# Transposing the attention weights on TensorE, redividing PSUM for the sums, and moving one normalisation past the MLP weight loads, in a one-core Trainium2 transformer block

## The chip, the core and the metric

The kernel runs on one NeuronCore of a Trainium2 chip. The engines are named as the profile names them: PE is TensorE (PEld its weight loads), DVE is VectorE, ACT is ScalarE, POOL is GpSimd, and SP is SyncE, which here only issues DMA transfers. Each engine works through its own queue in order, and semaphores tie the queues together. The metric is the device time of one execution in microseconds (us).

## The reference

The block is a pre-norm attention layer with softmax feature maps (linear attention), followed by an MLP whose input is normalised twice. S = 2048 rows, D = 576, H = 32 heads of width 18, F = 4608, all in bf16.

```python
def _A_ref(x, wqkv, w_phi, wo):
    qkv = (x @ wqkv) -> q, k, v per head
    pq = einsum("bhsd,hdf->bhsf", q, w_phi);  pk = the same of k
    phi_q = concat([softmax(pq), softmax(-pq)]);  phi_k = the same of pk
    kv = einsum("bhsf,bhsd->bhfd", phi_k, v);  z = einsum("bhsf->bhf", phi_k)
    num = phi_q @ kv;  den = phi_q . z + 1e-6
    return (num / den) @ wo

def _B_ref(x, w1, b1, w2, b2):
    y = layernorm(x)
    return gelu(y @ w1 + b1) @ w2 + b2

h  = x + _A_ref(layernorm(x), ...)
h2 = h + _B_ref(layernorm(h), ...)
```

## The kernel before

The 2048 rows are 16 tiles of 128 (`t`), four to a block `b`. The 32 heads are in 5 groups `g` of 7, 7, 7, 7 and 4 heads, that is of 126 (the last of 72) columns. PE and POOL run in the order in which the program writes their work, to the end of the kernel; ACT, DVE and SP do so up to `front.close()`, after which a planner orders them.

**Weights and normalisation (0 to about 17 us).** `x` comes in four loads. `wv`, the value weights, is loaded by `load_rows`: rows on partitions, in two transfers, and a third of a row (1152 bytes) at a time. The key and query weights are needed with their columns on partitions, because `fold` multiplies them by `bd`, a block-diagonal matrix of the head maps `w_phi` that POOL builds in `spread`. `load_turned` therefore loads them as `wkT` and `wqT` with five transposing DMAs each. `fold` makes `wkp` and `wqp`, the weights with the head maps multiplied in, one 128-row chunk `c` per call: six matmuls into a PSUM tile `pW`, then one copy to SBUF. `measure` takes the mean and variance of a tile on DVE (`bn_stats` twice, `bn_aggr`, and the one-column step `va`) and the inverse root `rs` on POOL; `scale` writes the normalised rows `lnb` on DVE. Tiles 0 to 3 are turned on PE (`transpose_to`), tiles 4 to 15 by a DMA on SP's queue, into `lnT`.

**The key loop (about 17 to 69 us).** For each tile `key` is ten matmuls into `pk`, two exponentials on ACT (`phik`), and a sum and a reciprocal on DVE (`sk`, `rk`). `value` is ten matmuls into `pv` and one copy on ACT (`vf`). `weigh` makes `vs` = `vf` * `rk` twice (for the two signs), on POOL, and for sign 0 of the last two tiles on DVE. From tile 6 on, each step also holds one `ask`: five matmuls of 512 columns for one (block, group) of the queries into `pq`, and two exponentials on ACT (`eT`). There are 20 asks. In the loop are also the two stages of `fold` for the query weights (at t = 3 and 4), and the measuring and scaling of later tiles.

**Sums and attention chain (about 69 to 102 us).** `sums(g, s)` accumulates over the 16 tiles into `pkv`; two DVE instructions (L405, L411) mask it into `kvm`. `combine(t, u)` takes tile t and one of two units of groups (0 to 2, or 3 and 4): matmuls into `pn`, two small copies on ACT (`sw`), a product on DVE (`tt`), a sum on POOL (`uu`), and, when its returned function is called, a division on DVE (`rec`, `ob`). `turn`, `residual`, `rescale` and `turn2` take a finished tile through the output projection (`pa`), the residual, the two normalisations and a transpose into `ln2T`.

**The MLP.** Eight slices of 256 rows; each is 324 matmuls into `ph` with `w1` (`up`), then four accumulations of 36 matmuls into `po` with `w2` (`down`). The attention work of later tiles is hung between the `po` matmuls by a table of marks. Every `po` accumulation needs all of `w2`; its first 18 matmuls use quarters 0 and 2, its last 18 quarters 1 and 3.

**Memory.** In PSUM the pool `two` has three buffers of two banks (`pw`, `pW`, `pk`, `pv`, `pkv`, `pn`, `pa`) and `one` has two buffers of one bank (`pT`, `pq`, `pb1`) until the MLP begins. In SBUF, `w1` and `w2` (41.5 KB per partition each) begin where the pool `kpool` lay, with all `phik` (36.9 KB) and `vs` (38.9 KB). So `w1` can be loaded once `sums(4, 1)` has read these, and `w2` reaches about 7 KB beyond, into the place of `tf_pool`, where the `tt` tiles of the first five `combine` calls lie; the last of these is `d20 = combine(2, 0)`. The loads are eight transfers of `w1` (L575; each fills 64 partitions) and then four of `w2` (L578; 128 partitions), all on SP's queue.

Of the kernel before, what the change touches and what calls it, by code (L numbers as in the profile page):

```python
# [8 lines left out]
P = 128  # L9
# [6 lines left out]
D = 576  # L16
# [21 lines left out]
def kernel(  # L38
# [65 lines left out]
    wkT = wpool.tile([P, NG, D], BF16, name="wkT", tag="wkT")  # L104
    wqT = wpool.tile([P, NG, D], BF16, name="wqT", tag="wqT")
# [4 lines left out]
    lnb = [wpool.tile([P, DP], BF16, name=f"lnb{i}", tag=f"lnb{i}") for i in range(4)]  # L110
# [5 lines left out]
    def load_turned(dst, first):  # L116
        for g in range(NG):
            f0 = first + g * 126
            nc.sync.dma_start_transpose(dst[:, g : g + 1, :], A_wqkv[:, f0 : f0 + P])

    wphi_rows = A_w_phi.rearrange("h d f -> (h d) f")
# [5 lines left out]
    nc.sync.dma_start(xh[:, 1:4, :], x_v[:, 1:4, :])  # L127
    load_rows(wv, A_wqkv[:, 2 * D : 3 * D])
    nc.sync.dma_start(xh[:, 4:8, :], x_v[:, 4:8, :])
    load_turned(wkT, D)  # L130
    load_turned(wqT, 0)
# [16 lines left out]
    nc.vector.memset(wv[64:P, 4, :], 0.0)  # L148
    for i in range(4):
        nc.vector.memset(lnb[i][:, D:DP], 0.0)  # L150
# [20 lines left out]
    def inverse(mv, n, bias, scale):  # L171
        va = small.tile([P, 2], FP32, name="va", tag="va")
        nc.vector.tensor_scalar(va[:, 0:n], mv[:, 0:n, 1], scale, bias, ALU.mult, ALU.add)  # L173
        rs = small.tile([P, 2], FP32, name="rs", tag="rs")
        nc.gpsimd.tensor_tensor(rs[:, 0:n], va[:, 0:n], mhalf[:, 0:n], ALU.pow)  # L175
        return rs

    def statistics(tiles, bias, scale):
        n = len(tiles)
        mv = small.tile([P, 2, 2], FP32, name="mv", tag="mv")  # L180
        for i, t in enumerate(tiles):
            st = small.tile([P, 2, nc.vector.BN_STATS_DIM], FP32, name="st", tag="st")
            nc.vector.bn_stats(st[:, 0, :], xh[:, t, 0:HALF])
            nc.vector.bn_stats(st[:, 1, :], xh[:, t, HALF:D])
            nc.vector.bn_aggr(mv[:, i, :], st[:, :, :])
        return mv, inverse(mv, n, bias, scale)
# [9 lines left out]
    def measure(*tiles):  # L196
        mv, rs = statistics(tiles, EPS, 1.0)
        for i, t in enumerate(tiles):
            moments[t] = (mv, rs, i)
# [5 lines left out]
    def scale(t):  # L205
        normalise(lnb[t % 4][:, 0:D], xh[:, t, :], *moments[t])
        if t >= 4:
            nc.sync.dma_start_transpose(turned(t), lnb[t % 4][:, :])
# [14 lines left out]
    def fold(wT, wp, c, copy):  # L223
        m = P if c < NC - 1 else 64
        pW = two.tile([P, 2, 512], FP32, name="pW", tag="two")
        for i, off, g, lo, hi in BITS:
            k = P if g < NG - 1 else 72
            nc.tensor.matmul(
                pW[:m, i, off : off + hi - lo],
                wT[:k, g, c * P : c * P + m],  # L230
                bd[:k, g, :, :].rearrange("p h f -> p (h f)")[:, lo:hi],
                start=True, stop=True,
            )
        copy(wp[:m, c, 0:D].rearrange("p (i f) -> p i f", i=2), pW[:m, :, 0:HALF])

    eT = {}

    def ask(b, g):
        if g == 0:
            eT[b] = e_pool.tile([P, NG, 2, 512], BF16, name="eT", tag="eT")  # L240
        pq = one.tile([P, 512], FP32, name="pq", tag="one")
        for c in range(NC):
            nc.tensor.matmul(  # L243
                pq[:, :], wqp[:, c, g * 126 : g * 126 + P], lnT[b][:, c, :],
                start=(c == 0), stop=(c == NC - 1),
            )
        nc.scalar.activation(eT[b][:, g, 0, :], pq[:, :], AF.Exp, scale=1.0)
        nc.scalar.activation(eT[b][:, g, 1, :], pq[:, :], AF.Exp, scale=-1.0)  # L248
# [43 lines left out]
    warm(40)  # L292
# [4 lines left out]
    warm(8)  # L297
    measure(2)
    scale(1)
    transpose_to(lnb[1], turned(1))  # L300
    value(0)
    spread(0)
    measure(3)
    scale(2)
    transpose_to(lnb[2], turned(2))
    value(1)
    spread(1)
    spread(2)
    measure(4, 5)
    scale(3)  # L310
    transpose_to(lnb[3], turned(3))
    value(2)
    spread(3)
    spread(4)
    value(3)
    scale(4)
    scale(5)
    fold(wkT, wkp, 0, nc.scalar.copy)
    fold(wkT, wkp, 1, nc.vector.tensor_copy)
    fold(wkT, wkp, 2, nc.scalar.copy)  # L320
    fold(wkT, wkp, 3, nc.vector.tensor_copy)
    fold(wkT, wkp, 4, nc.scalar.copy)
# [4 lines left out]
    asked = iter([(b, g) for b in range(NT // 4) for g in range(NG)])  # L327
    for t in range(NT):
        key(t)
        if t == 0:  # L330
            scale(6)
            scale(7)
        if t in (3, 4):
            for c in ((0, 1), (2, 3, 4))[t - 3]:
                fold(wqT, wqp, c, nc.scalar.copy)
        if t >= 6:
            ask(*next(asked))
# [30 lines left out]
    more = lambda: ask(*next(asked))  # L368
    more()
    more()  # L370
    inner.close()

# [18 lines left out]

    def sums(g, s):
        n = GH[g]
        m = P if g < NG - 1 else n * DH
        pkv = two.tile([P, 7 * VW], FP32, name="pkv", tag="two")
# [20 lines left out]
    banks = {}  # L416

    def bank(shape, dtype, name):
        pool, tag = banks["one"]
        return pool.tile(shape, dtype, name=name, tag=tag)  # L420
# [56 lines left out]
    def residual(t):  # L477
        st = small.tile([P, 2, nc.vector.BN_STATS_DIM], FP32, name="st", tag="st")
        mv = small.tile([P, 2, 2], FP32, name="mv", tag="mv")
        for i in range(2):  # L480
            cs = slice(i * HALF, (i + 1) * HALF)
            pool, tag = banks["pa"]
            pa = pool.tile([P, HALF], FP32, name="pa", tag=tag)
            for c in range(NC):
                nc.tensor.matmul(  # L485
                    pa[:, :], oTs[t][:, c, :], wo[:, c, cs],
                    start=(c == 0), stop=(c == NC - 1),
                )
            nc.vector.tensor_tensor(xh[:, t, cs], pa[:, :], xh[:, t, cs], ALU.add)  # L489
            nc.vector.bn_stats(st[:, i, :], xh[:, t, cs])  # L490
# [8 lines left out]
    def turn2(t):  # L499
# [8 lines left out]
        for c0, c1 in ((0, 5), (5, KC)):  # L508
# [3 lines left out]
            copy = nc.vector.tensor_copy if c0 else nc.scalar.copy  # L512
            copy(dst[:, c0:c1, :], pT[:, 0 : c1 - c0, :])
# [6 lines left out]
    banks["one"] = (one, "one")  # L520
    banks["two"] = (two, "two")

    banks["pa"] = (two, "two")
    banks["tt"] = tf_pool

    sums(0, 0)
    sums(0, 1)
    sums(1, 0)
    sums(1, 1)
    sums(2, 0)  # L530
    sums(2, 1)
    sums(3, 0)
    d00 = combine(0, 0)
    sums(3, 1)
    d10 = combine(1, 0)
    d00()
    more()
    turn_b1()
    more()
    sums(4, 0)  # L540
    d10()
    sums(4, 1)
    kctx.close()
    d01 = combine(0, 1)
# [3 lines left out]
    more()  # L548
    more()
    turn(0)  # L550
    turn(1, nc.vector.tensor_copy)
    more()
    m0 = residual(0)
    m1 = residual(1)
    more()
    rescale(0, *m0)
    more()
    turn2(0)
    rescale(1, *m1)
    more()  # L560
    turn2(1)
    d20 = combine(2, 0)
    d20()
# [13 lines left out]
    for q in (0, 2, 1, 3):  # L577
        nc.sync.dma_start(w2[:, 9 * q : 9 * q + 9, :], w2v[:, 9 * q : 9 * q + 9, :])  # L578
    psA.close()
    front.close()  # L580

    pn_pool = ctx.enter_context(
        tc.tile_pool(name="pn_pool", bufs=1, space=bass.MemoryType.PSUM, reuse_waits="tile")
    )
    acc = ctx.enter_context(
        tc.tile_pool(name="acc", bufs=6, space=bass.MemoryType.PSUM, reuse_waits="tile")
    )
    banks["one"] = (acc, "acc")
    banks["two"] = (pn_pool, "pn")

    banks["pa"] = (acc, "acc")
# [70 lines left out]

    for s_ in range(NS):
        mlp(s_)
# [31 lines left out]
```

## Time and profile before

| | |
|---|---|
| median of three runs | 427.08 us (427.08 to 427.48) |
| the profiled execution | 426.47 us |
| its span, from the first instruction to the last | 424.8 us |
| busy share of PE / PEld / ACT / DVE / POOL | 94% / 77% / 45% / 43% / 25% |
| PE work of the two MLP products, `ph` and `po` | 143.1 and 151.1 us |
| DMA moved | 27.08 MB |

Two lines of the profile's table of 40 slices (10.6 us each) say where DMA counts; a digit is the busy share in tenths, and the second line is the rate in each slice:

```profile
DMA  9762140099990320121032004101210220030000
GB/s 218 138 156 40 34 110 0 2 189 208 256 346 9 71 46 3 29 58 32 2 57 60 3 3 85 31 2 29 59 31 3 56 63 3 2 71 15 2 2 28
```

DMA is busy in two places: in the first three slices, when inputs and attention weights arrive, and in slices 9 to 12 (85 to 127 us), when the MLP weights do. PE's clock is granted in full but for two stretches of 3.41 us, from 98.50 and from 129.22 us, in which it is at half.

### The profile page before, as it was taken

What the parts mean: (1) busy time and instruction counts of PE and PEld (TensorE: products, weight loads), DVE (VectorE), ACT (ScalarE), POOL (GpSimd) and SP (SyncE); (2) the same over time, 40 slices, a digit from 0 to 9 for tenths busy, and PEclk for the clock granted to TensorE, in tenths of its full rate; (3) what the DMA queues carried; (4) which work ended last, traced back from release to release, by engine and by line L of the source; (5) the groups of instructions that cost most, each with busy time, mean ns of one, the idle gap of its engine ahead of it and who ended that gap; (6) DMA issues with size and microseconds to landing.
All of it is one profiled execution on the core that took longest, in us unless ns stands there. A gap on an engine that the chain in (4) does not pass through costs nothing.

```text
span 424.8 us, 11023 instructions
## 1 busy us (share of the span) xinstructions
PE 400.6 (94%) x4811; PEld 325.9 (77%) x4811; DVE 182.1 (43%) x397; ACT 191.5 (45%) x460; POOL 106.2 (25%) x139
## 2 busy tenths in 40 slices
PE   7879998886988899999999999999999999999997
PEld 6656666744966688788888888887888888878875
DVE  6689998664024630750174046206601740330000
ACT  3678775255851148107601840481067018404810
POOL 5258798112011320141023004101410240011000
PEclk9999999998998999999999999999999999999999
DMA  9762140099990320121032004101210220030000
GB/s 218 138 156 40 34 110 0 2 189 208 256 346 9 71 46 3 29 58 32 2 57 60 3 3 85 31 2 29 59 31 3 56 63 3 2 71 15 2 2 28
DMA packets 53130, 27.08 MB, mean 64 GB/s; under 512 B 40026, under 2 KB 52698, under 8 KB 52954
## 3 DMA queue, kind: packets, MB, share of 16 engines
q1 hardware_dynamic: 52480, 26.36, 27.4%
q8 instruction: 37, 0.61, 0.6%
q10 hardware_dynamic: 602, 0.02, 0.1%
q14 instruction: 11, 0.09, 0.1%
HBM read 14.48 MB, written 2.36 MB: 40 GB/s over the span
## 4 chain that ended last, share of the span: by engine, by line
PE 80%; DMA 6%; DVE 5%; SPq 3%; ACT 2%; issue 1%; POOL 1%; DVEq 0%; ACTq 0%; POOLq 0%
PE po L629 32%; PE ph L602 29%; PE pa L485 4%; PE pq L243 4%; PE pv L253 4%; PE pk L253 4%; DMA w<-in_B_w_dram 3%; SPq L578 2%; PE pkv L397 2%; PE pn L434 2%; DMA xh<-in_A_x_dram 2%; DMA lnT<-lnb 1%; DVE tt L445 1%; DVE vs L286 1%; POOL uu L451 1%
## 5 line engine op out<-in xcount | busy, mean ns | idle before, releaser
L629 PE MATMUL po<-w,h 128*128 128x288 bf16 x1152 | 151.1, 288 | 3.7 <-DMA w<-in_B_w_dram 3.7
L608 ACT ACTIVATE h<-ph,b1col 128x256 bf16<-128x256 f32 x288 | 120.9, 471 | 72.0 <-PE ph L602 52.9
L602 PE MATMUL ph<-ln2T,w 64*128 64x256 bf16 x2592 | 143.1, 269 | 1.8 <-DVE tt L445 1.4
L602 PEld LDWEIGHTS <-w 64*128 64x128 bf16 x2592 | 126.8, 94 | 17.7 <-issue 3.7
L629 PEld LDWEIGHTS <-h 128*128 128x128 bf16 x1152 | 111.2, 98 | 32.8 <-issue 5.6
L489 DVE TENSOR_TENSOR xh<-pa,xh 128x288 bf16<-128x288 f32 x32 | 14.4, 449 | 110.6 <-PE pa L485 110.6
L175 POOL TENSOR_TENSOR rs<-va,mhalf 128x1 f32<-128x1 f32 (+1 forms) x26 | 15.5, 594 | 163.4 <-DVE va L173 163.1
L442 ACT COPY sw<-pn 128x21 f32<-128x21 f32 (+1 forms) x32 | 5.5, 173 | 98.9 <-PE pn L434 98.9
L451 POOL TENSOR_TENSOR uu<-tt 128x399 f32<-128x399 f32 (+1 forms) x32 | 26.4, 826 | 84.1 <-DVE tt L445 82.3
L253 PEld LDWEIGHTS <-lnT 128*128 128x128 bf16 x320 | 31.0, 98 | 12.2 <-DMA lnT<-lnb 2.5
L286 POOL TENSOR_TENSOR vs<-vf,rk 128x608 bf16<-128x608 bf16 x30 | 36.8, 1253 | 7.0 <-DVE rk L281 5.8
L633 DVE TENSOR_TENSOR ot<-po,hb 128x288 bf16<-128x288 f32 x32 | 14.5, 454 | 52.7 <-PE po L629 52.7
L445 DVE TENSOR_TENSOR tt<-pn,sw 128x798 f32<-128x798 f32 (+1 forms) x32 | 25.1, 786 | 22.9 <-ACT sw L443 22.8
L619 POOL TENSOR_TENSOR hb<-xh,b2bc 128x576 f32<-128x576 bf16 x16 | 20.4, 1272 | 53.2 <-DVE ot L633 53.2
L243 PE MATMUL pq<-lnT,wqp 128*128 128x512 bf16 x100 | 25.2, 389 | 1.8 <-ACT eT L248 1.1
L253 PE MATMUL pk<-wkp,lnT 128*128 128x288 bf16 x160 | 21.7, 286 | 2.3 <-DMA lnT<-lnb 2.3
L253 PE MATMUL pv<-wv,lnT 128*128 128x288 bf16 x160 | 22.1, 286 | 0.1
L485 PE MATMUL pa<-wo,oT 128*128 128x288 bf16 x160 | 22.1, 286 | 0.0
L272 ACT ACTIVATE phik<-pk 128x576 bf16<-128x576 f32 x32 | 19.1, 649 | 6.4 <-PE pk L253 6.0
L277 DVE TENSOR_REDUCE sk<-phik 128x64 f32<-128x1152 bf16 x16 | 21.2, 1327 | 0.1
L456 DVE TENSOR_TENSOR ob<-uu,rec 128x378 bf16<-128x378 f32 (+1 forms) x32 | 20.3, 633 | 1.1
L189 DVE TENSOR_SCALAR ln<-xh,mv,rs 128x576 bf16<-128x576 bf16 x32 | 16.8, 569 | 7.0 <-POOL rs L175 7.0
(70 smaller groups left out, 240.1 us busy)
## 6 DMA issues: line engine op xcount, KB each, us to landing
w<-in_B_w_dram SPq DMA_DIRECT2D x8, 648.0 KB, 15.7
w<-in_B_w_dram SPq DMA_DIRECT2D x4, 1296.0 KB, 16.2
out_dram<-ot SPq DMA_DIRECT2D x16, 144.0 KB, 1.8
xh<-in_A_x_dram SPq DMA_DIRECT2D x1, 1152.0 KB, 6.3
wv<-in_A_wqkv_dram SPq DMA_DIRECT2D x1, 576.0 KB, 6.2
xh<-in_A_x_dram SPq DMA_DIRECT2D x1, 576.0 KB, 6.8
wo<-in_A_wo_dram SPq DMA_DIRECT2D x1, 576.0 KB, 4.2
xh<-in_A_x_dram SPq DMA_DIRECT2D x1, 432.0 KB, 3.4
```

What stands on the lines that cost most here:

```text
L243: nc.tensor.matmul(pq[:, :], wqp[:, c, g * 126 : g * 126 + P], lnT[b][:, c, :], start=(c == 0), stop=(c == NC - 1),)
L253: nc.tensor.matmul(dst[:, i, 0:HALF], lhs[:, c, :], w[:, c, i * HALF : (i + 1) * HALF], start=(c == 0), stop=(c == NC - 1),)
L277: nc.vector.tensor_reduce(sk[:, :], phik[t][:, :, :].rearrange("p s (h f) -> p (s h) f", f=DH), AX.X, ALU.add)
L286: eng.tensor_tensor(vs[t][:, s, :, :], vf[t % 4][:, :, :], rk[t][:, s, :].rearrange("p (h o) -> p h o", o=1).to_broadcast([P, NH, VW]), AL ...
L445: nc.vector.tensor_tensor(tt[:, :, 0:nh, :], pnv[:, :, :, 0:VW], sw[:, :, 0:nh].rearrange("p s (h o) -> p s h o", o=1).to_broadcast([P, 2, ...
L451: nc.gpsimd.tensor_tensor(uu[:, 0:nh, :], tt[:, 0, 0:nh, :], tt[:, 1, 0:nh, :], ALU.add)
L456: nc.vector.tensor_tensor(o[:, h0 * DH : (h0 + nh) * DH].rearrange("p (h d) -> p h d", d=DH), uu[:, 0:nh, 0:DH], rec[:, 0:nh].rearrange("p ...
L485: nc.tensor.matmul(pa[:, :], oTs[t][:, c, :], wo[:, c, cs], start=(c == 0), stop=(c == NC - 1),)
L602: nc.tensor.matmul(ph[half][:, :], w1[rows, c, p_ * P : (p_ + 1) * P], x[rows, c, :], start=(c == 0), stop=(c == KC - 1),)
L608: nc.scalar.activation(h1[m // 9][:, m % 9, :], ph[half][:, :], AF.Gelu_apprx_tanh, bias=b1col[:, m : m + 1], scale=1.0,)
L619: nc.gpsimd.tensor_tensor(hb[:, :], xh[:, t, :], b2bc[:, :], ALU.add)
L629: nc.tensor.matmul(po[:, :], h1[m // 9][:, m % 9, i_ * P : (i_ + 1) * P], w2[:, m, cs], start=(n == 0), stop=(n == NM - 1),)
```

## The change

- The key and query weights are loaded by `load_rows`, as `wv` is, into two of the four `eT` buffers, which nobody needs so early. The order on SP's queue is x (tile 0), x (1 to 3), `wk`, `wv`, x (4 to 7), `wq`, x (8 to 15). A new function `flip` turns one group of columns on PE (five transposes into a PSUM tile of pool `two`) and copies it into one shared tile `wT`, on ACT or DVE.
- The order of the start is new: flips of `wk` stand between the transposes of the first tiles, folds between the values; the measuring of tiles 4 and 5 moves from before the scaling of tile 3 to after the last fold; `value(3)` moves to after `key(0)`. The five flips of `wq` stand at t = 1 and 2, its folds at t = 3 (three) and t = 4 (two). The first warm-up has 46 transposes in place of 40, the second (8) is gone. `lnb` has six buffers in place of four. From tile 4 on, the one-column step `va` is POOL's.
- After the key loop PSUM is divided anew: `pair_pool` (two buffers of two banks, for `pn`), `free_pool` (two of one bank, for `pkv`, `pT`, `pb1`, `pa`) and `ask_pool` (two of one bank, for `pq`).
- The order of sums, asks and combines is new: `combine(0, 0)` and `combine(1, 0)` come before `sums(3, 0)`, an ask before them; one ask is split round the `combine` of the second units; both `rescale` calls come together.
- `combine(2, 0)` moves from before the MLP weight loads to after them, past the twelve issues on SP's queue and past the closing of the PSUM pools; its `tt` then lies in `tt_pool`.

The core of the diff:

```diff
-    wkT = wpool.tile([P, NG, D], BF16, name="wkT", tag="wkT")
-    wqT = wpool.tile([P, NG, D], BF16, name="wqT", tag="wqT")
+    wT = wpool.tile([P, NG, D], BF16, name="wT", tag="wT")
...
+    load_rows(wk, A_wqkv[:, D : 2 * D])
     load_rows(wv, A_wqkv[:, 2 * D : 3 * D])
     nc.sync.dma_start(xh[:, 4:8, :], x_v[:, 4:8, :])
-    load_turned(wkT, D)
-    load_turned(wqT, 0)
+    load_rows(wq, A_wqkv[:, 0:D])
...
-    def inverse(mv, n, bias, scale):
+    def inverse(mv, n, bias, scale, eng=nc.vector):
-        nc.vector.tensor_scalar(va[:, 0:n], mv[:, 0:n, 1], scale, bias, ALU.mult, ALU.add)
+        eng.tensor_scalar(va[:, 0:n], mv[:, 0:n, 1], scale, bias, ALU.mult, ALU.add)
...
+    def flip(w, g, copy):
+        m = P if g < NG - 1 else 72
+        pX = two.tile([P, DP], BF16, name="pX", tag="two")
+        for c in range(NC):
+            nc.tensor.transpose(
+                pX[:m, c * P : (c + 1) * P], w[:, c, g * 126 : g * 126 + m], ident[:, :]
+            )
+        copy(wT[:m, g, :], pX[:m, 0:D])
...
+    warm(46)
     measure(0); measure(1); scale(0); transpose_to(lnb[0], turned(0))
+    flip(wk, 0, act); measure(2); scale(1); flip(wk, 1, dve)
+    transpose_to(lnb[1], turned(1)); spread(0..2)
+    flip(wk, 2, act); measure(3); scale(2); flip(wk, 3, dve)
+    transpose_to(lnb[2], turned(2)); flip(wk, 4, act); spread(3); spread(4)
+    value(0); scale(3); fold(wkp, 0, act); transpose_to(lnb[3], turned(3))
+    fold(wkp, 1, dve); value(1); fold(wkp, 2, act); fold(wkp, 3, dve)
+    value(2); fold(wkp, 4, act)
+    measure(4, 5); scale(4); scale(5); measure(6, 7)
...
     for t in range(NT):
         key(t)
         if t == 0:
             scale(6)
             scale(7)
+            value(3)
+        if t in (1, 2):
+            for g in ((0, 1, 2), (3, 4))[t - 1]:
+                flip(wq, g, act)
         if t in (3, 4):
-            for c in ((0, 1), (2, 3, 4))[t - 3]:
-                fold(wqT, wqp, c, nc.scalar.copy)
+            for c in ((0, 1, 2), (3, 4))[t - 3]:
+                fold(wqp, c, act)
...
+    psA.close()
+    pair_pool = psum_pool(psB, "pair_pool", 2)
+    free_pool = psum_pool(psB, "free_pool", 2)
+    ask_pool = psum_pool(psB, "ask_pool", 2)
...
     sums(0, 0) ... sums(2, 1)
-    sums(3, 0); d00 = combine(0, 0); sums(3, 1); d10 = combine(1, 0); d00()
-    more(); turn_b1(); more(); sums(4, 0); d10(); sums(4, 1)
+    more(); d00 = combine(0, 0); d10 = combine(1, 0); sums(3, 0); d00()
+    turn_b1(); sums(3, 1); d10(); more(); sums(4, 0); sums(4, 1)
     kctx.close()
...
-    d20 = combine(2, 0)
-    d20()
     fore.close()
...
+    combine(2, 0)()
     for s_ in range(NS):
         mlp(s_)
```

(Calls are put on one line here where the diff has one to a line.)

## The prediction

> **What bounds the kernel now.** I read the chain of waits first, backwards: which wait ends last in each stage. Its rows are start, length (us), engine, work, line.
>
> ```profile
> 65.18 1.19 ACT phik L272 x2
> ...
> 67.37 1.88 DVE vs L286
> ...
> 71.27 0.87 DVE vs L286
> 72.18 5.99 PE pkv L397 x97
> ...
> 105.00 0.39 SPq L578
> ...
> 115.37 13.83 DMA w<-in_B_w_dram
> 129.24 2.32 PE po L629 x9
> ```
>
> From 129.24 to the span's end at 424.8 the chain is almost all PE: 295.6 us in which the change alters nothing but names of pools. What releases PE at 129.24 is the last quarter of `w2`. Before that, the sums waited until 72.18 for DVE's last `vs`.
>
> Next, the busy times by stretches of 2 us: length, then PE, PEld, DVE, ACT, POOL, the clock, the DMA share and GB/s.
>
> ```profile
> 88.00:90.00 2.00, 1.21 (x12) 0.77 (x12) 0.96 (x3) 1.55 (x3) 0.00 (x0) 1.00 1.08 209
> ...
> 104.00:106.00 2.00, 2.00 (x40) 2.00 (x38) 0.96 (x2) 0.91 (x3) 2.00 (x2) 1.00 1.08 215
> ...
> 110.00:112.00 2.00, 2.00 (x42) 2.00 (x38) 0.00 (x0) 1.72 (x5) 0.00 (x0) 1.00 1.09 192
> ...
> 114.00:116.00 2.00, 1.60 (x31) 1.29 (x27) 0.00 (x0) 1.54 (x4) 0.00 (x0) 1.00 1.07 353
> ...
> 126.00:128.00 2.00, 0.00 (x0) 0.00 (x0) 0.76 (x3) 0.00 (x0) 1.02 (x1) 1.00 0.67 216
> ```
>
> The DMA engines are full from 88 to 126 without a hole. `w1` (576 x 4608 x 2 bytes = 5.31 MB) runs at about 205 GB/s, 26 us; then `w2`, as large, at 356, 15 us; with start and tail 44.7 us from the first issue (84.54, right after the last `pkv`) to 129.24. So the end is **t_w + 44.7 + 295.6**, where t_w is the moment at which `sums(4, 1)` frees `w1`'s place, as long as PE reaches the 19th matmul of the first `po` before the load does. It does: it stood there 3.3 us. Everything between t_w and that point goes into that wait.
>
> Last, the start, from the timeline of PE and ACT (in brackets: idle time before, and what ended it):
>
> ```profile
> 25.11 1.40 PE L253 MATMUL pk<-wkp,lnT 128*128 128x288 bf16 x10 [2.33 <-DMA lnT<-lnb]
> 26.54 1.19 ACT L272 ACTIVATE phik<-pk 128x576 bf16<-128x576 f32 x2 [2.01 <-PE pk L253]
> 27.62 1.70 ACT L234 CAST wqp<-pW 128x576 bf16<-128x576 f32 x3
> 27.78 0.44 PE L228 MATMUL pW<-bd,wqT 128*64 128x126 bf16 x6 [0.73 <-ACT phik L272]
> 28.32 1.39 PE L253 MATMUL pv<-wv,lnT 128*128 128x288 bf16 x10
> ```
>
> `key(4)` waits for a DMA that stood on SP's queue behind ten transposing loads; then a third `pW` waits for a buffer of `two` until ACT has done both exponentials of `pk`. From 28.32 PE has no hole until 69.44.
>
> **The change, part by part.** I laid each engine's queue out in program order with the durations of these rows, up to t_w.
>
> *Free place of w2.* SP waited 5.4 us for `combine(2, 0)` before the first `w2` issue (105.00). In the change it issues at once. Worth nothing: `w1` is still moving at 192 to 216 GB/s until 112, so `w2` only queues sooner. The cover is `w1`'s own transfer; were it gone, up to 5.4 us would show.
>
> *Loads.* SP loses ten transposing issues (7.52 + 7.03 us) and gains four plain ones (about 0.5 each). So x (8 to 15) and the transposes of tiles 4 and on are no longer late: the waits of 2.33 us (PE) and 1.08 us (DVE for x) go. What is late next is `wk`: it stands where `wv` stood (issues at 1.71 and 2.18, landing 6.2 and 6.1 later), so the first flip starts at about 8.1, and it holds up the transposes of tile 1 behind it on PE, which `scale(1)` has ready by 7.8.
>
> *Start until key(0).* A flip costs PE 0.29 us (five transposes: `pT` at 12.22, the next matmul at 12.51) and 0.54 to 0.59 us on ACT (`vf` to `wkp` start to start; `lnT`) or 0.45 on DVE. Flips 0 and 1 and `pT(1)` 8.1 to 8.9; flips 2 and 3 to 9.6; DVE copies flip 1, measures tile 3 and scales tile 2 until 10.8 (1.09 + 0.07 + 0.42 after the copy); `pT(2)`, flip 4, `pv(0)` to 12.7; then folds (0.27 each), `pT(3)` and two more values (1.225 each) with waits of 0.1 and 0.4 for PSUM: `key(0)` at 17.3, against 17.16. No change.
>
> *From key(0) to value(4).* Before: 17.16 to 28.32, 11.2 us. After, PE's work is five keys and `value(3)` (6 x 1.225 = 7.35), five flips (1.43) and five folds (1.35): 10.1 us. But `two` has three buffers, and the third small tile behind a key waits until ACT has read that key: the key's tail 0.17, two exponentials 1.19, two semaphores 0.1, less the two flips or folds already issued, 0.55: 0.9 us (the trace's gap there, from the second fold's last start to 27.78, is the same). This happens four times (flips after `key(1)`, `key(3)` behind flip 4, folds after `key(3)`, `value(4)`), twice with a further 0.27 for a copy, and 0.2 for `wkp`'s last chunk: 4.4 us. So value(4) starts at 17.3 + 14.5 = 31.8, **3.5 us late**. Bounds: without any of these waits 27.4 (0.9 us early); with the copies at `vf`'s whole 0.64, 32.1.
>
> *To the sums.* PE's 41.1 us follow (28.32 to 69.44), then 15 `pkv` (0.9): the 16th is ready at 73.9 instead of 70.3. DVE is no longer last there: it is spared the wait for x and six `va` steps (0.17 three times, then 0.67, 0.90, 0.95: 3.0 us), so `vs` of tile 15 is there by about 73. On POOL a `va` isn't in the trace: between DVE's undisturbed 0.17 and the 0.70 of `rs`; I take 0.35, being nearer the plain step; POOL has room (32.3 us busy of the 38 from 30 to 68), so nothing at either end. Net: 72.18 becomes 73.9, **+1.7**.
>
> *Sums and chain to t_w.* Before, 72.18 to 84.5: 12.3 us, with one wait of note, the second ask, 1.05 us for a buffer of `one` until its exponentials were done. Ask buffers of their own remove it. But `pkv` now has two buffers in place of three, shared with `pb1`, and on DVE's queue the masking of `sums(3, 0)` stands behind two `tt`:
>
> ```profile
> 78.87 0.99 DVE L445 TENSOR_TENSOR tt<-pn,sw 128x798 f32<-128x798 f32 x1 [0.27 <-ACT sw L443]
> 80.18 0.99 DVE L445 TENSOR_TENSOR tt<-pn,sw 128x798 f32<-128x798 f32 x1
> 82.11 1.24 PE L243 MATMUL pq<-lnT,wqp 128*128 128x512 bf16 x5 [1.05 <-ACT eT L248]
> ```
>
> After the 16th matmul at 73.9: five groups (0.95 each) to 78.7, an ask (1.08) to 79.8, two `pn` (0.37 each), `sums(3, 0)` and `pb1`: PE is ready for `sums(3, 1)` at 81.5. Its buffer: ACT does the ask's exponentials until 81.0, `sw` to 81.25, `tt` twice to 83.2, the mask (0.38) to 83.6. A wait of 2.1 us. Then 0.95 + 1.08 + 1.2: t_w = 87.1. The section costs +2.1 - 1.05, less 0.2 of smaller gaps, **+0.8**.
>
> *After t_w.* Fewer gaps, no `tt` ahead of the first `ph` (1.37 us before): PE arrives 2 to 3 us sooner after t_w than before, and waits that much longer. Nothing.
>
> Sum: 1.7 + 0.8 = +2.5 on the span of 424.8, 427.3; the profiled execution was 426.47 and the median of the runs 427.08, so I forecast **429.6**. Own range: +1.0 (half of the PSUM waits shorter) to +4.3 (a clock window worse).
>
> *The clock.* It fell at 98.50 for 3.41 us, although PE's longest hole before was 1.56 us; the window before it held 1.25 us of PE work in 3.41:
>
> ```profile
> 9.76:13.17 3.41, 2.17 (x21) 1.57 (x20) 2.72 (x9) 2.09 (x4) 1.80 (x5) 1.00 0.91 189
> ...
> 95.09:98.50 3.41, 1.25 (x12) 0.66 (x11) 2.54 (x7) 2.18 (x4) 0.56 (x1) 1.00 1.09 203
> ```
>
> The new start has a window near 1.75 us of 3.41 (6.4 to 9.8), between these two. If it falls, some 3 us of PE work take twice as long, and 1.3 to 1.8 us reach t_w. The restart at the `w2` wait runs at half clock for one window (129.22 to 132.63) already; there it can go 0.9 us either way.
>
> [...]
>
> **Rivals.**
> *w2 overlaps w1* (faster). If the queued `w2` filled what `w1` leaves, 10.6 MB at 356 GB/s take 29.8 us, PE would set the end (it needs some 38 us from t_w, against 44.7): 429.6 - 6.7 = 422.9. For it: `w1` is slow with the engines full. Against: from 105 to 112 `w2` was queued behind `w1` and the rate stayed at 192 to 216. 8%.
> *The PSUM waits don't come* (faster). `value(4)` at 27.4; then DVE decides: from its last fold copy (15.8) 12 measurings at 1.09, 12 scalings at 0.75, 16 sums and reciprocals at 1.83, two `vs` (2.75) and 1.5 of rest come to 71.4, 0.7 before 72.13. If `sums(3, 1)` also finds its buffer, 1.05 more: 425.3. It needs both, against the order on DVE's queue. 12%.
> *One of them* only: about 427.3, no change. 14%.
> *Forecast plus a clock window*: 431.2. 12%.
> The forecast itself: 54%.
>
> **How the numbers follow.** 0.2% (0.9 us) is about what a measurement of this kernel can tell from no change. Faster: 8 + 12 = 20%; same 14%; slower 54 + 12 = 66%. The range for eight in ten, from the faster case of 425.3 to the clock case with its 0.9: 425.3 to 432.1.
>
> **What would show it.** Right: `value(4)` near 32 with PE waiting for `phik` four times before; no wait for `vs` at the sums; PE waiting about 2 us for DVE's mask before `sums(3, 1)`; first `w` issue near 87; `w2` issues directly behind `w1`'s, and yet the same 44.7 us to the `po` wait, which is longer. Wrong: a first issue before 84.5, or less than 44 us from it to the last landing.

## The result, and the profile after

| | before | after |
|---|---|---|
| median of six runs each, us | 427.08 (425.85 to 428.32) | 428.88 (428.50 to 430.14) |
| ratio to before, 95% interval | | 1.0046 [1.0023, 1.0068] |
| span of the profiled execution, us | 424.8 | 426.8 |
| `value(4)` starts | 28.32 | 31.06 |
| 16th `pkv` (all `vs` are there) | 72.18 | 73.06 |
| t_w, first issue of `w1` | 84.54 | 85.99 |
| first issue of `w2` | 105.00 | 100.15 |
| last wait of PE for `w2` ends | 129.24 | 131.04 |
| PE's waits for `w1` and `w2` in all | 3.7 | 6.95 |

The change makes the kernel slower by 1.8 us, a little under half a per cent. The span grew by 2.03 us: 1.45 up to t_w, 0.35 from t_w to the end of the wait for `w2` (44.70 became 45.05), and 0.23 behind it (295.52 became 295.75).

The timeline of PE in the changed kernel (start, length, what, and in brackets the idle time before and what ended it) shows the new waits of the start and where the loads are waited for:

```profile
22.01 0.44 PE L229 MATMUL pX<-ident,eT 128*128 128x128 bf16 x5 [0.72 <-ACT phik L291]
25.20 1.39 PE L272 MATMUL pk<-wkp,lnT 128*128 128x288 bf16 x10 [0.72 <-ACT phik L291]
27.87 0.44 PE L239 MATMUL pW<-bd,wT 128*128 128x126 bf16 x6 [0.73 <-ACT phik L291]
31.06 1.39 PE L272 MATMUL pv<-wv,lnT 128*128 128x288 bf16 x10 [0.61 <-ACT phik L291]
...
115.52 5.09 PE L632 MATMUL ph<-ln2T,w 64*128 64x256 bf16 x89 [1.21 <-DMA w<-in_B_w_dram]
123.85 2.84 PE L659 MATMUL po<-w,h 128*128 128x288 bf16 x15 [2.82 <-DMA w<-in_B_w_dram]
131.04 1.75 PE L659 MATMUL po<-w,h 128*128 128x288 bf16 x9 [2.92 <-DMA w<-in_B_w_dram]
```

Four times PE stands until ACT has read a key, because the third tile behind that key finds no buffer of `two`: a flip at 22.01, the next key at 25.20, a fold at 27.87, a value at 31.06. Later it waits three times for weights, the first time inside the first MLP product.

The chain of waits of the changed kernel (start, length, engine, work, line) shows the second cost, at the sums:

```profile
80.40 0.87 issue
81.27 0.98 DVE tt L489
82.25 0.20 DVE kvm L454
82.44 0.11 DVE kvm L460
...
82.59 1.12 PE pkv L446 x16
83.72 1.08 PE pq L258 x5
84.80 1.12 PE pkv L446 x32
...
116.23 14.76 DMA w<-in_B_w_dram
...
131.04 1.75 PE po L659 x9
```

`sums(3, 1)`, at 82.59, waited 1.73 us for the mask of `sums(3, 0)` (L454, L460), which stood behind two `tt` of 0.9 to 1.0 on DVE. Before t_w the chain of the kernel before ran through `vs` and had no mask in it. Its end is the same in both kernels: the last quarter of `w2`, then PE.

SP's queue in the changed kernel shows the two groups of weight loads (start and length of the group of issues):

```profile
85.99 14.06 SPq L611 DMA_DIRECT2D w<-in_B_w_dram  x8
100.15 20.88 SPq L614 DMA_DIRECT2D w<-in_B_w_dram  x4
```

`w2` now follows `w1` at once: its first issue no longer waits for `combine(2, 0)`. The stretches of 2 us (busy time of PE, PEld, DVE, ACT and POOL, then the clock, the DMA share and GB/s) say what that brought:

```profile
104.00:106.00 2.00, 2.00 (x42) 2.00 (x38) 0.66 (x1) 1.71 (x5) 0.25 (x1) 1.00 1.09 209
112.00:114.00 2.00, 2.00 (x41) 2.00 (x38) 0.00 (x0) 1.72 (x5) 0.00 (x0) 1.00 1.09 190
116.00:118.00 2.00, 2.00 (x42) 1.79 (x38) 0.00 (x0) 1.25 (x4) 0.00 (x0) 1.00 1.06 347
126.00:128.00 2.00, 2.00 (x12) 1.44 (x11) 0.28 (x1) 0.26 (x2) 0.00 (x0) 0.50 1.09 361
```

With `w2` queued since 100.15, the rate is still about 200 GB/s until `w1` is through, and only then 350. The load as a whole is about as long as before. The last line shows PE's clock at half while the load still runs; it is so for 3.41 us from 124.84, and again from 131.66, behind the last wait.

### The profile page after: what moved, and what is told of

The parts are those of the page before. It is cut to its first block, busy times and chain, and to the rows that moved or that the text cites. A ratio compares the mean times of both kernels' runs of the same rounds, so it can differ in the third digit from the quotient of the medians.

```text
span 426.8 us, 11124 instructions
## 1 busy us (share of the span) xinstructions
PE 403.7 (95%) x4859; PEld 329.1 (77%) x4859; DVE 180.9 (42%) x397; ACT 195.5 (46%) x468; POOL 107.9 (25%) x145
## 4 chain that ended last, share of the span: by engine, by line
PE 83%; DMA 5%; DVE 4%; SPq 3%; ACT 2%; issue 1%; POOL 1%; POOLq 0%; DVEq 0%
PE po L659 31%; PE ph L632 29%; PE pk L272 5%; PE pv L272 5%; PE pq L258 4%; PE pa L528 4%; DMA w<-in_B_w_dram 3%; SPq L614 3%; PE pkv L446 2%; PE pn L478 2%; DMA eT<-in_A_wqkv_dram 1%; DVE tt L489 1%; ACT phik L291 1%; POOL uu L495 1%; DVE st L533 1%
## 5 line engine op out<-in xcount | busy, mean ns | idle before, releaser
L663 DVE TENSOR_TENSOR ot<-po,hb 128x288 bf16<-128x288 f32 x32 | 14.5, 454 | 52.6 <-PE po L659 52.6
```

## The experiments

Each kernel was run in several rounds beside the kernel before; medians are in us, ratios are to the kernel before on the same chip, with the 95% interval, and times at a place are those of the profiled execution. Two cautions for reading them. The kernel before had a median of 427.08 beside the changed kernel and of 427.16 to 427.76 in these later rounds, so that up to 0.7 us of a difference to 428.88 may be the round's. And t_w differs from execution to execution: in the seven traces with the changed kernel's start, `key(0)` begins between 16.39 and 17.66. Behind `key(0)` the seven repeat each other: 14.18 to 14.19 us to `value(4)`, and 42.00 from there to the 16th `pkv`. Lengths of sections can be compared far more closely than moments.

**The place of w2 alone.** The kernel before, with only `combine(2, 0)` moved behind the loads.

```diff
-    d20 = combine(2, 0)
-    d20()
     fore.close()
...
+    combine(2, 0)()
     for s_ in range(NS):
         mlp(s_)
```

> The kernel before with one part of the change: combine(2, 0) stands behind the MLP weight loads, so that the place of w2 is free early. Theory (the load runs without a hole from t_w and sets the end): the first w2 issue comes at about 99.6 us instead of 105.0, the last quarter still lands 44.7 us after the first w1 issue at 84.5, PE waits for it until 129.2, and the time is 427.1 (within 0.5). Rival (the 5.4 us that SP waited were time lost): the last landing comes up to 5.4 us sooner and the time is 422 to 426.

427.99 against 427.56, ratio 1.0012 [0.9999, 1.0025]: no gain. SP's queue:

```profile
85.15 15.20 SPq L573 DMA_DIRECT2D w<-in_B_w_dram  x8
100.45 19.18 SPq L576 DMA_DIRECT2D w<-in_B_w_dram  x4
```

The first `w2` issue comes at 100.45 instead of 105.00, and yet the last quarter is there 44.83 us after t_w (44.70 before). The stall of SP was covered by `w1`'s own transfer. (This t_w is 0.6 later than that of the kernel before, though the two kernels are the same up to there. In both, the sums wait for DVE's `vs`, and DVE had waited for x (8 to 15), which was there at 24.95 in this execution and at 24.38 in that of the kernel before; from then to the 16th `pkv` it is 47.8 us in both.)

**The start alone.** The kernel before with the new loads, flips, folds and the order up to the end of the key loop.

```diff
+    load_rows(wk, A_wqkv[:, D : 2 * D])
...
-    load_turned(wkT, D)
-    load_turned(wqT, 0)
+    load_rows(wq, A_wqkv[:, 0:D])
...
+        if t in (1, 2):
+            for g in ((0, 1, 2), (3, 4))[t - 1]:
+                flip(wq, g, act)
```

> The kernel before with the new start alone: weights loaded by rows and turned on TensorE, the new order to the end of the key loop, va on POOL; sums, PSUM division and attention chain as before. Theory: value(4) starts near 31.1 (28.3 before) with PE waiting for phik behind each key, the 16th pkv comes at 73.1 (72.18 before) without a wait for vs, the old order then takes 12.3 us, the first w1 issue is at 85.4 and the time is about 0.9 above before: 428.0. Rival A (the new start costs nothing, as DVE set the sums): 427.1. Rival B (all of the 1.8 comes from here): 428.9.

428.37 against 427.56, ratio 1.0023 [1.0005, 1.0041]. `value(4)` starts at 30.58 and the 16th `pkv` at 72.58, t_w is 84.82.

```profile
71.70 6.74 PE L426 MATMUL pkv<-vs,phik 128*128 128x133 bf16 x112
82.38 1.24 PE L258 MATMUL pq<-lnT,wqp 128*128 128x512 bf16 x5 [1.05 <-ACT eT L267]
```

On PE's timeline the sums run through without a wait for `vs`: PE, late by the start, sets their begin. The second ask's 1.05 us is still there. So the start by itself takes time. Its sections are those of the changed kernel (14.19 and 42.00 us); that t_w is only 0.28 later than in the kernel before comes from an early `key(0)`, 16.39 (16.88 in the changed kernel).

**The tail alone.** The kernel before with the new PSUM pools, order of sums and asks, and place of `combine(2, 0)`.

```diff
-    sums(3, 0)
+    more()
     d00 = combine(0, 0)
-    sums(3, 1)
     d10 = combine(1, 0)
+    sums(3, 0)
     d00()
...
+    turn_b1()
+    sums(3, 1)
+    d10()
```

> The kernel before with the second half of the change alone: the new PSUM division and order of sums, asks and combines, and combine(2, 0) behind the loads; the old start. Theory: the 16th pkv still waits for vs until 72.2; sums(3, 1) then waits about 1.7 us for a buffer that DVE frees behind two tt, the wait of 1.05 for the second ask is gone, the first w1 issue is at 85.1 (0.55 late) and the time is 427.6. Rival A (all of the 1.8 comes from here): 428.9. Rival B (the new order gains, and the start costs more than the whole): below 427.0.

428.01 against 427.56, ratio 1.0014 [0.9999, 1.0029]; t_w is 84.67.

```profile
71.62 5.04 PE L429 MATMUL pkv<-vs,phik 128*128 128x133 bf16 x81 [0.64 <-DVE vs L294]
81.28 1.12 PE L429 MATMUL pkv<-vs,phik 128*128 128x133 bf16 x16 [1.73 <-DVE kvm L443]
```

The wait for the mask is here to the hundredth, 1.73, and the section from the 16th `pkv` to t_w takes 13.05 (12.36 before). But t_w hardly moves, because DVE's `vs`, which still sets the 16th `pkv`, was 0.56 earlier in this execution: x (8 to 15) was there at 23.79 in place of 24.38. (The wait for `vs` is 0.64 in place of 1.70 because PE was also 0.5 later; its clock was at half for 3.41 us from 24.67.) The interval of this ratio holds 1, so that the tail's cost is shown by the section, not by the time. The two halves' medians, +0.8 and +0.45, add up to less than the whole's +1.8 by an amount that their intervals cover.

**More work behind t_w.** The changed kernel with 60 transposes that nothing reads right behind the last sums.

```diff
     kctx.close()
+    pw = bank([P, P], BF16, "pw")
+    for _ in range(60):
+        nc.tensor.transpose(pw[:, :], ident[:, :], ident[:, :])
```

> The changed kernel with 60 more transposes of the identity on TensorE right behind the last sums (60 x 0.056 = 3.4 us of work that nothing reads). Theory: PE reaches the w2 wait some 3 us later and waits that much less; last landing and time as in the changed kernel, 428.9 (within 0.4). Rival (the chain behind the sums sets the end, not the load): 3.4 us more, 432.3.

429.19 against 427.56, ratio 1.0037 [1.0024, 1.0050]; the changed kernel's own was 1.0046 [1.0023, 1.0068].

```profile
85.38 3.52 PE L581 MATMUL pw<-ident 128*128 128x128 bf16 x60
...
131.15 2.32 PE L662 MATMUL po<-w,h 128*128 128x288 bf16 x9 [3.72 <-DMA w<-in_B_w_dram]
```

3.52 us of work on PE, and the wait for `w2` ends where it did (131.15; 131.04), with t_w at 85.61. The rival's 3.4 us more did not come: work of this size between t_w and that wait costs nothing, and the formula with t_w holds.

**The start without its waits for PSUM.** The changed kernel with flips and folds of the query weights set one at a time behind a key or a value, not two or three behind one key.

```diff
         if t == 0:
             scale(6); scale(7)
+            flip(wq, 0, act)
             value(3)
-        if t in (1, 2):
-            for g in ((0, 1, 2), (3, 4))[t - 1]:
-                flip(wq, g, act)
-        if t in (3, 4):
-            for c in ((0, 1, 2), (3, 4))[t - 3]:
-                fold(wqp, c, act)
+            flip(wq, 1, act)
+        if t in (1, 2, 3):
+            flip(wq, t + 1, act)
+        if t in (4, 5, 6):
+            fold(wqp, 2 * t - 8, act)
...
+        if t in (4, 5):
+            fold(wqp, 2 * t - 7, act)
```

(In the diff two calls are put on one line, and the ask of t = 6 comes behind its value.)

> The changed kernel with the flips and folds of the query weights spread out, one behind each key or value from t = 0 on, so that none has to wait for a buffer that ACT is still reading. Theory (the 0.72 us waits behind the keys delay the stream, and DVE, which had 1.3 us to spare at the last tiles, sets the sums next): value(4) starts near 26.5 (31.06 in the changed kernel), the 16th pkv comes at about 71.8 (73.06) behind a wait for vs, the first w1 issue at 84.7 and the time is about 1.3 below the changed kernel. Rival A (TensorE's work for the flips is the price): no change. Rival B (the whole 3 to 4 us come through): 425.5.

426.69 against 427.76, ratio 0.9982 [0.9967, 0.9997]: 2.2 us less than the change, and a little faster than the kernel before (1.3 us less than the change had been expected). `value(4)` starts at 26.50, 4.6 us sooner; of that, folds moved behind it are some 1.1 (four of 0.27 each). Then DVE is last again:

```profile
71.03 5.04 PE L450 MATMUL pkv<-vs,phik 128*128 128x133 bf16 x81 [0.78 <-DVE vs L305]
```

The 16th `pkv` comes 2.03 us sooner than in the changed kernel, t_w 1.90 sooner.

**The sums without their wait.** The changed kernel with `sums(3, 0)` and `sums(3, 1)` ahead of the first combines, and `turn_b1` behind the last sums.

```diff
-    for g in range(3):
+    for g in range(4):
         for s in range(2):
             sums(g, s)
...
     d10 = combine(1, 0)
-    sums(3, 0)
     d00()
-    turn_b1()
-    sums(3, 1)
     d10()
...
     sums(4, 1)
+    turn_b1()
```

> The changed kernel with sums(3, 0) and sums(3, 1) before the first combine and the turn of b1 behind the last sums, so that no accumulation waits for a buffer behind two tt on DVE. Theory: the section from the 16th pkv to the first w1 issue takes 11.1 us (12.9 in the changed kernel, 12.4 before), the first w1 issue comes 1.8 sooner, the last landing too, and the time is about 1.8 below the changed kernel, near the kernel before. Rival (TensorE's order behind the sums matters, the chain being moved later by the same amount): no change.

427.29 against 427.76, ratio 0.9977 [0.9962, 0.9992]. The section from the 16th `pkv` to t_w takes 10.90 in place of 12.93; t_w is 83.81.

```profile
72.03 7.69 PE L446 MATMUL pkv<-vs,phik 128*128 128x133 bf16 x128
...
86.75 0.17 PE L559 MATMUL pb<-ident,b1nat 36*128 36x36 bf16 x1 [3.01 <-DVE kvm L460]
```

All eight of the first `sums` run together, and what waits now (3.01 us, for a buffer of `free_pool`) is behind t_w, where it costs nothing. Of the 2.2 us won at t_w 1.8 reach the end of the wait for `w2` in the profiled execution (129.21), and 1.0 of them is lost again behind it, where the clock was at half for two windows of 3.41 us, not one. The medians differ by 1.6.

**Both together.** The two edits above in one kernel.

> Both of the edits above that shorten the way to the last sums (small tiles spread out; sums(3) before the combines). Theory: the gains add, as both move the first w1 issue: about 83 (85.99 in the changed kernel), the last landing 45 us later, 3 us below the changed kernel and 1.3 below the kernel before. Rival: DVE takes back one of them, and the time is that of the better one alone.

424.45 against 427.76, ratio 0.9931 [0.9911, 0.9952], t_w 81.89: 4.4 us under the change. The gains at t_w, 1.90 and 2.18, add up: t_w is 4.10 sooner than in the changed kernel. In the profiled execution, the longest of the six (425.87), 3.2 of these reach the end of the wait for `w2` (127.81). The time is lower than expected, and DVE takes neither gain back. Both costs of the change are waits for PSUM buffers, and both go by order alone.

**w1 on two queues.** The changed kernel, with the transfers to the upper 64 partitions issued on ACT's queue, beside SP's to the lower 64.

```diff
     for q in range(4):
         cs = slice(q * FF // 8, (q + 1) * FF // 8)
         for half in range(2):
-            nc.sync.dma_start(w1[half * KH : (half + 1) * KH, :, cs], w1v[half, :, :, cs])
+            eng = nc.scalar if half else nc.sync
+            eng.dma_start(w1[half * KH : (half + 1) * KH, :, cs], w1v[half, :, :, cs])
```

(`w1` has a pool of its own right behind the last sums, so that ACT's issues stand early on its queue.)

> The changed kernel with the four second halves of w1 issued on ACT's queue and the four first halves on SP's, all right behind the last sums (w1 in a pool of its own). Theory A (a w1 transfer fills only 64 partitions and runs at 205 GB/s for that reason; two queues side by side fill all 128 and run at 356): all of w is there about 34 us after the first issue in place of 45, TensorE then sets the end, and the time is 421 to 423. Theory B (all transfers share the same 16 engines, which are full already): the load takes the same 45 us and the time is 428.9 (within 0.5). In both the load from the last sums on is what sets the end.

422.61 against 427.76, ratio 0.9887 [0.9864, 0.9909], with the same t_w (86.00). The stretches of 2 us, the last two figures being DMA share and GB/s:

```profile
94.00:96.00 2.00, 2.00 (x10) 1.05 (x9) 0.00 (x0) 0.74 (x2) 0.00 (x0) 0.65 1.09 385
...
118.00:120.00 2.00, 2.00 (x41) 2.00 (x38) 0.00 (x0) 1.69 (x5) 0.00 (x0) 1.00 0.52 175
```

From 90 to 104 the weights move at 308 to 385 GB/s with the same share of 1.08 to 1.11, all of them are there by 120, and PE waits for none: t_w to the 19th `po` matmul is 39.64 us, PE's own work.

**Two queues, the same half.** Is it the second queue, or that both halves of the partitions are written at once? In the first test each queue fills the lower half and then the upper of one quarter of the columns, and so on.

```diff
-    for q in range(4):
+    for q in (0, 2, 1, 3):
...
-            eng = nc.scalar if half else nc.sync
+            eng = nc.scalar if q >= 2 else nc.sync
```

> As the kernel with two queues, but the w1 transfers are dealt out so that both queues fill the same 64 partitions at a time: SP takes the first two column chunks, ACT the last two, each the first half of the partitions and then the second. Theory (64 partitions at a time are what makes w1 slow): the rate stays near 205 GB/s while w1 moves, the load takes about 45 us from the last sums and the time is near the changed kernel's, 428.9. Rival (two queues move more than one, wherever they write): about 356 GB/s and the 422.6 of the kernel with two queues.

425.44 (424.12 to 430.13) against 427.63, ratio 0.9959 [0.9932, 0.9987]: between the two, and spread wide; the 428.9 that my theory gave is missed in the median. In the profiled execution (429.06) the rate is 192 to 202 GB/s while `w1` moves, with three stretches of 260 to 276:

```profile
92.00:94.00 2.00, 1.44 (x10) 1.05 (x11) 1.37 (x4) 1.12 (x2) 0.28 (x1) 0.50 1.08 196
94.00:96.00 2.00, 2.00 (x7) 0.76 (x5) 0.13 (x1) 0.23 (x1) 0.00 (x0) 0.50 1.09 260
...
100.00:102.00 2.00, 1.61 (x8) 0.52 (x6) 1.87 (x6) 1.43 (x3) 0.41 (x2) 1.00 1.09 272
...
104.00:106.00 2.00, 1.46 (x18) 1.13 (x17) 0.49 (x2) 1.45 (x4) 0.00 (x0) 1.00 1.09 192
106.00:108.00 2.00, 1.66 (x32) 1.66 (x33) 0.99 (x1) 1.97 (x5) 0.38 (x1) 1.00 1.09 276
```

Nothing holds the queues in step here, so at times one may have been at the lower half while the other was at the upper; no trace shows which half was being filled. That left the median open, and the next kernel closes this gap: both queues fill the lower half in all their quarters first, then the upper.

```diff
-    for q in (0, 2, 1, 3):
-        for half in range(2):
+    for half in range(2):
+        for q in (0, 2, 1, 3):
```

> Changed kernel with w1 again on two queues (SP has the first two column quarters, ACT the last two), but now each queue first fills partitions 0 to 63 in all its quarters and then 64 to 127, so that the queues can't drift onto different halves except for a moment in the middle. If two queues help only because they write both halves of the partitions at once (my theory): the rate stays at 190 to 215 GB/s from the first issue (about 86) for some 26 us, to about 112, then 350 with w2; the last transfer lands 44 to 45.5 us after the first issue and the time is that of the changed kernel or, because the first MLP matmul waits for the second half of w1, up to 2 us above: 428 to 431 us. If a second queue helps by itself: 330 to 380 GB/s from the first issue on, all weights there by about 119, and 422 to 425 us.

427.85 (426.17 to 429.50) against 427.35, ratio 1.0001 [0.9981, 1.0021]: the gain of the two queues is gone; the median is 0.15 under the range that I had given. The stretches of 2 us:

```profile
94.00:96.00 2.00, 2.00 (x7) 0.62 (x6) 0.49 (x1) 0.26 (x1) 0.00 (x0) 0.50 1.08 196
...
104.00:106.00 2.00, 1.11 (x17) 0.94 (x15) 0.42 (x1) 1.77 (x5) 0.00 (x0) 1.00 1.09 199
110.00:112.00 2.00, 1.48 (x16) 1.03 (x18) 0.00 (x0) 0.00 (x0) 0.00 (x0) 0.50 1.09 205
...
116.00:118.00 2.00, 1.28 (x24) 1.15 (x26) 0.00 (x0) 0.92 (x3) 0.00 (x0) 1.00 1.08 343
```

Two queues, and 192 to 209 GB/s as with one (243 once, near the middle), until `w2` with its 128 partitions comes; the load is through at about 130, some 44 us after its first issue (86.73). The time alone would not show this, because in this order PE also waits for the upper half of `w1` inside the first product, and afterwards no more for `w2`:

```profile
110.52 5.43 PE L636 MATMUL ph<-ln2T,w 64*128 64x256 bf16 x72 [4.31 <-DMA w<-in_B_w_dram]
```

The rates do show it: with two queues on one half `w1` moves at 192 to 209 GB/s, with one on each half at 308 to 385, so that it is slow with the half and not with the number of queues. One thing goes along with the half in all these kernels: the two halves of the partitions hold the two halves of `w1`'s columns, so that no run separates where the data lands from where in memory it is read. `w2`, read in pieces of the same 1152 bytes on one queue, moved at 332 to 362 GB/s into all 128 partitions (116 to 130 here), which speaks for the partitions.

**All of it.** The kernel with both orders mended, plus the two queues, with ACT's four issues spread between the work of the chain so that they don't hold it up (in the kernel with two queues alone PE had waited 3.43 us at one place, 0.49 in the changed kernel), and `turn_b1` just before `turn2`.

```diff
+    for q_ in range(4):
+        load_w1(nc.sync, 0, q_)
...
+    load_w1(nc.scalar, 1, 0)
...
+    load_w1(nc.scalar, 1, 3)
```

> All that shortened the way, together: small tiles spread out, sums(3) before the combines, the second halves of w1 on ACT's queue, here one at a time between ACT's other work, and the turn of b1 just before the first turn2. Theory: first w1 issue at about 82, all of w there 36 to 37 us later (the second halves start late), TensorE reaches the 19th matmul of the first po at about 118 to 119.5 and no longer waits there; the time is 414 to 417. Rival (ACT's issues hold up the chain behind the sums as they did with two queues, 3.4 us at one place): 418 to 420.

419.65 against 427.63, ratio 0.9820 [0.9794, 0.9845]. The 414 to 417 that I had expected is missed; the time is in the rival's range. Two lines of PE's timeline say why:

```profile
84.93 0.80 PE L482 MATMUL pn<-kvm,eT 128*128 128x80 bf16 x6 [2.37 <-DVE kvm L464]
...
123.91 1.26 PE L671 MATMUL po<-w,h 128*128 128x288 bf16 x9 [1.14 <-DMA w<-in_B_w_dram]
```

The combine behind the last sums waits 2.37 us for its mask, since `d10` stands ahead of it on DVE, and with ACT's issues spread the transfers lie side by side for a part of the time only (191 to 218 GB/s from 86 to 94, 258 to 358 from there to 114), so that PE waits for `w2` again. The hold-up by ACT's issues that the rival named is not among PE's waits here. The clock fell, too, at 84.70 and at 98.35.

The last kernel moves `d10()` behind the last sums and issues two of ACT's transfers at once, while ACT has nothing else.

```diff
-    d10()
     sums(4, 0)
     sums(4, 1)
+    d10()
...
+    for q_ in range(2):
+        load_w1(nc.scalar, 1, q_)
```

> The kernel with everything together, with two edits behind the first w1 issue: the division of tile 1 stands behind the last sums, so that DVE masks sums(4, 0) and sums(4, 1) first (pn waited 2.37 us for that mask), and two of the second halves of w1 go out on ACT's queue at once while ACT is idle (82.0 to 85.4), in place of one at 85.8 and one at 89.0. Theory (with two queues the load no longer has time to spare, and TensorE's way behind the sums and the load both count): the pn wait falls to about 1 us, all of w is there at 120 to 121 in place of 123.9, and the time is 416.5 to 418.5. Rival (TensorE alone sets the end now): 2.4 us less at most from pn, but the same if the clock falls again behind it: 419 to 420.

417.26 (416.04 to 417.57) against 427.16, ratio 0.9766 [0.9749, 0.9782]: in the expected range, and the best of all kernels here, 2.3% under the kernel before and 2.7% under the changed one (417.26 / 428.88 = 0.973). PE's timeline:

```profile
84.06 0.60 PE L482 MATMUL pn<-kvm,eT 128*128 128x80 bf16 x6 [1.58 <-DVE kvm L464]
...
119.84 1.63 PE L671 MATMUL po<-w,h 128*128 128x288 bf16 x12
```

The wait for the mask is 1.58 where about 1 was expected, there is none for `w2`, t_w to the 19th `po` matmul is 38.13, and the clock does not fall within the span of this execution. What each of the two edits brought was not separated.

## Why the prediction was right, step by step

**The formula.** t_w + 44.7 + 295.6 was right. In the nine traces whose `w1` goes through SP's queue alone, t_w to the end of the wait for `w2` is 44.68 to 45.91 us, although t_w lies between 81.89 and 85.99, and 3.52 us of extra work behind t_w did not move the end. The 44.7 was 0.35 short for the changed kernel, and the 295.6 about 0.2. What the 0.35 is made of was not tried; the two shortest (44.68 and 44.70) are those in which `w2` is issued late.

**The free place of w2: nothing.** Right, shown by the kernel with that edit alone. The rival that `w2` would fill what `w1` leaves was rightly held small, by the row that showed both queued at 200 GB/s. But the prediction had no cause for the slow `w1`; in the runs it goes with the half that is filled at a time (187 to 218 GB/s, against 308 to 385 with both). Why `w2`, queued behind `w1` on one queue, did not fill the rest was not tried by itself. The 422.9 that this rival gave to a load at the full rate is near the 422.61 that two queues reached.

**The start until key(0): no change.** Right: 16.88 against the forecast 17.3; `wk` landed in time for a first flip at 7.39, not 8.1. In the seven traces with this start it is 16.39 to 17.66, so that the good fit of one execution is in part luck.

**From key(0) to value(4): +3.5.** Right in the mechanism, too large in size: +2.74. Of the 0.74 too much, 0.42 was won before `key(0)`; the section itself took 14.18 us where 14.5 was added up. The four waits came where they were put, at 0.61 to 0.73 us, 2.78 in all, where 0.9 each was charged. The 0.9 counts from the start of the last matmul of the fold; the row that it was checked against has 0.73 of idle time. The smaller gaps, 1.27 in place of 0.74, took back a part of the difference. That taking these waits away moves the 16th `pkv` by 2.03 and t_w by 1.90 shows that they, and not the PE work added, made the start slow (PE's work is the same there).

**To the sums: +1.7.** It was +0.88, and the whole difference is that of `value(4)`: from there to the first `pkv` took 41.13 us (41.1 forecast). DVE is no longer last, as said. `va` on POOL takes 0.19 us, not 0.35, and nothing hangs on it.

**Sums and chain: +0.8.** It was +0.57. The wait at `sums(3, 1)` stood where it was forecast, behind two `tt` and a mask, and lasted 1.73 in place of 2.1; the second ask's 1.05 went. The two mis-sized terms are thus the waits behind the keys and the wait for this mask: t_w moved by 1.45, not by 2.5.

**After t_w: nothing.** Right, since the load sets the end. PE was at the first `ph` 14.71 us after t_w, 4.6 sooner than before (19.30), where 2 to 3 had been forecast. Its waits for weights grew by only 3.2 us, because the clock was at half for 3.41 us from 124.84: by estimate that cost PE some 1.6 us before the end of the wait for the load (half of the 3.27 us that it was busy in that window), and nothing at the end.

**The clock.** The front did not fall to half in the changed kernel, nor in the kernel with its start alone. In the old start it did so in two executions (from 8.73 with the place of `w2` alone, from 24.67 with the tail alone) and not in that of the kernel before, so that such a window is no matter of the order alone. The 1.56 us were the longest hole in the window before 98.50, not the longest before it: PE had stood 2.33 us before 25.11 with the clock in full. The work in a window, as the prediction read it, does fit: in the 3.41 us before a fall PE had worked 1.25 us (kernel before, 98.50), 1.25 and 1.20 (the two old starts) and 0.99 and 0.62 (changed kernel, 124.84 and 131.66), while 1.72 us in the window from 23.41 of the kernel before brought none. In the new start the two windows from 5.37 held 2.47 and 2.35 us, not the 1.75 that was feared. The forecast of one window, up to 0.9 either way, at the wait for `w2` held: 295.75 behind it.

In sum 1.05 too much at t_w, 0.35 and 0.23 too little behind it, and 0.2 between the spans' difference (2.03) and the medians' (1.80) make the 0.7 us by which 429.6 lies above 428.88. That errors of both signs cancel in part is luck; the mechanism of each part is not.

## What to carry to other kernels

Look for the load that everything before a late wait flows into: as long as that wait lasts only what moves the load's first issue counts or shortens the load (4.10 us at t_w were 4.4 us of time here), and work put behind that issue is free until the wait is used up (3.52 us of it left the wait's end at 131.15, against 131.04). A tile that shares a pool of three buffers with a slowly read one waits as soon as two more small ones stand between (0.61 to 0.73 us each time here); set such steps one at a time between the large ones. And when the DMA engines count as full at half the rate of the next transfer (about 205 and 355 GB/s here, both at a share near 1.08), ask which partitions each transfer fills before believing that the time is the bytes'.

## What the chip showed that was not expected

**Half the partitions, half the rate.** 187 to 218 GB/s with transfers to 64 partitions at a time (up to 240 in the first 5 us of the load), at a DMA share of 1.06 to 1.11, whether one queue issues them or two that keep to the same half (243 once there); 308 to 385 with one queue on each half, at the same share. From the one queue to the two on both halves the rate rose by some 70% (205 to about 350) and the time fell by 6.3 us (428.88 to 422.61). What holds the rate down at one half no run shows.

**The clock after a wait.** The stretch behind PE's last wait for `w2` took 295.5 to 295.8 us when the clock was at half for one window of 3.41 us there, 296.3 to 296.8 with two windows in a row (6.83 us), and 294.1 to 294.2 in the three kernels where it did not fall there (two of these have no such wait; it is counted from their 19th `po` matmul). Which of the first two comes goes with the moment of the fall: in the five traces with two windows the clock had fallen 1.3 to 2.2 us before PE's work began again, in the four with one it fell between 0.02 us before that and 0.62 us after.

**A small step that DVE sometimes takes long for.** `va` on two columns took 0.19 us on POOL in the changed kernel, all six times. On DVE in the kernel before it took 0.17 us three times, and 0.67, 0.90 and 0.95 us the other three. Each of these three ended 0.02 to 0.03 us after a pair of POOL's `vs` (which ended at 34.29, 42.28 and 50.31), as if held until then; no run tested it.
